# Attention over half batches of queries, interleaved with the feed-forward of the half batch before it

## The chip, the core and the metric

One Trainium2 chip, one of its cores. The metric is device time in microseconds (us), measured on the chip; lower is better. The engines named below are PE (TensorE: matmuls and transposes, with the weight loads as a row of their own), DVE (VectorE), ACT (ScalarE), POOL (GpSimd) and SP (SyncE, which here only issues DMAs). Each has its own queue and works it off in the order of the program.

## The reference

Hashed attention over 4 batches of 8 heads, 768 tokens and 64 channels, and then a gated feed-forward over the 3072 tokens of 512 channels that the heads make together:

```python
# attention: q, k, v (4, 8, 768, 64), proj (64, 6)
q_bits = (einsum('bhsd,dk->bhsk', q, proj) > 0)
k_bits = (einsum('bhsd,dk->bhsk', k, proj) > 0)
mask   = bucket(q_bits)[:, :, :, None] == bucket(k_bits)[:, :, None, :]   # all 6 bits agree
scores = where(mask, q @ k.T / sqrt(64), -1e9)
attn   = softmax(scores) @ v
# feed-forward: x (3072, 512) are the heads side by side
gelu   = gelu_erf(x @ w_gate)              # w_gate (512, 1536)
ffn    = (gelu * (x @ w_val)) @ w_out      # w_val (512, 1536), w_out (1536, 512)
out    = x + sigmoid(x @ w_res) * ffn      # w_res (512, 512)
```

All inputs are float32.

## The kernel before, in words

**Mask inside the matmul.** For each head there is a tile `aug` of 71 rows: 64 rows with the scaled channels of q (first 768 columns) and of k (next 768), 6 rows with the hash bits as +0.5 or -0.5, and a constant row (1 on the q side, -1.5 on the k side). One matmul over 71 rows gives the score plus a term that is zero where all bits agree and large and negative elsewhere, so Exp needs no mask. The constant row is written once by memsets (L82, L83) on DVE into the 12 buffers of `aug`; the memsets cover the bit rows too, which later DMAs overwrite.

**Preparing a pair of heads** (`prep_pair`, 16 pairs in all): POOL casts v into `vaug` (L141); PE transposes q and k in float32 in three groups of four (L148, tile `tps`); ACT copies groups 0 and 2 and DVE group 1 into `trT` (L150, L152); PE multiplies with `proj` (L156, tile `hps`); DVE makes the bits (L159); DVE writes the 64 channel rows of `aug` in bf16 (L163, four operations); SP issues eight small DMAs that move the bits to their rows (L170). Each `yield` ends a part; the main loop takes one part at a time.

**An attention step** (`scores`, then `attend` two steps later, `LEAD`): one block of 128 keys of one head against all 768 queries. PE: 512 + 256 columns into the tile `sc` (L183, L184, two buffers). ACT: Exp of 768 columns into `e` (L186). PE: six matmuls of 65 columns into `av` (L196, one buffer, 64 channels and the softmax sum for six blocks of queries). After the sixth block of keys DVE takes the reciprocal and writes `xtok` (L205, L206). A batch has 48 steps.

**Feed-forward of a batch.** `transpose_x` (PE L215 into `xps`, DVE L216 into `xT`), then all 24 gate groups (PE L223, four matmuls of 384 columns each; ACT Gelu L225) in one block, and then the generator `feed_forward`: for each half of the batch 12 items of `vps` (L233, four matmuls of 384) with a DVE product (L237), and for each of its three token blocks `rps` (L242), Tanh on ACT (L245, the sigmoid), `ops` (L249, twelve matmuls of 512 in three items), two DVE operations (`y` L254, `o` L256) and the output DMA on SP (L257). That makes 48 items. Tiles `tps`, `hps`, `xps`, `gps`, `vps`, `rps` and `ops` share three PSUM buffers.

**Order.** It is written out by hand: the program's order is each engine's order. Two pairs are prepared ahead of the loop. Batch 0's 48 steps have no feed-forward beside them; the weights (14 loads on SP in float32, L133, and a cast on POOL, L134) are brought in here, one in three steps, and the other pairs are prepared. In the steps of a later batch one or two items of the previous batch's `feed_forward` are issued per step, and the next batch's pairs are prepared in every second step. Then follow what is left of the generators, `transpose_x` and the 24 gate groups. The last batch's `feed_forward` comes after all attention.

Of the kernel before, what the change touches and what calls it, by code (L numbers as in the profile page):

```python
# [10 lines left out]
FP32 = mybir.dt.float32  # L11
BF16 = mybir.dt.bfloat16
AF = mybir.ActivationFunctionType
ALU = mybir.AluOpType
PSUM = bass.MemoryType.PSUM
# [3 lines left out]
def kernel(  # L19
# [24 lines left out]
    KAUG = D + NBITS + 1  # L44
# [12 lines left out]
    wstage = ctx.enter_context(tc.tile_pool(name="wstage", bufs=2))  # L57
    tr_pool = ctx.enter_context(tc.tile_pool(name="tr", bufs=2))
    e_pool = ctx.enter_context(tc.tile_pool(name="e", bufs=6))
    x_pool = ctx.enter_context(tc.tile_pool(name="x", bufs=2))  # L60
    h_pool = ctx.enter_context(tc.tile_pool(name="h", bufs=1))
# [5 lines left out]


    ident = const.tile([P, P], FP32, name="ident")
    make_identity(nc, ident)  # L70
    ident_bf = const.tile([P, P], BF16, name="ident_bf")
    make_identity(nc, ident_bf)
    proj_pair = const.tile([P, 32], FP32, name="proj_pair")
    nc.vector.memset(proj_pair, 0.0)
    nc.sync.dma_start(proj_pair[0:D, 0:NBITS], proj)
    nc.sync.dma_start(proj_pair[D:2 * D, NBITS:2 * NBITS], proj)

    NAUG = 12
    augs = []
    for i in range(NAUG):  # L80
        a = const.tile([P, 2 * S], BF16, name=f"aug{i}")
        nc.vector.memset(a[D:KAUG, 0:S], 1.0)  # L82
        nc.vector.memset(a[D:KAUG, S:2 * S], -0.25 * NBITS)  # L83
        augs.append(a)
    NVA = 2
    vaugs = []
    for i in range(NVA):
# [7 lines left out]

    staged = {}

    def load_pair(b, j):
        for nm, src in (("q", q), ("k", k), ("v", v)):
            s = stage.tile([P, 2, T, D], FP32, tag=nm + "s", name=nm + "s")  # L100
            nc.sync.dma_start(
                s, src[b, 2 * j:2 * j + 2].rearrange("h (p t) d -> p h t d", t=T))
            staged[(nm, b, j)] = s
# [6 lines left out]
    def load_weights():  # L110
        for dst, src in ((wg, moe_w_gate), (wv, moe_w_val)):
            for ko in range(KM):
                yield dst[:, ko, :], src[ko * P:(ko + 1) * P, :], None
        for k3 in range(KF // 3):
            yield (wo[:, 3 * k3:3 * k3 + 3, :],
                   moe_w_out[3 * k3 * P:(3 * k3 + 3) * P, :].rearrange("(c p) d -> p c d", p=P), 3)
        for k2 in range(KM // 2):
            yield (wr[:, 2 * k2:2 * k2 + 2, :],
                   moe_w_res[2 * k2 * P:(2 * k2 + 2) * P, :].rearrange("(c p) d -> p c d", p=P), 2)

    weight_gen = load_weights()

    def load_weight():
        nxt = next(weight_gen, None)
        if nxt is None:
            return
        dst, src, parts = nxt
        tmp = wstage.tile([P, DFF], FP32, tag="wtmp", name="wtmp")
        if parts is None:
            view = tmp  # L130
        else:
            view = tmp[:, :parts * DMODEL].rearrange("p (c d) -> p c d", c=parts)
        nc.sync.dma_start(view, src)  # L133
        nc.gpsimd.tensor_copy(dst, view)  # L134


    def prep_pair(b, j):

        qs, ks, vs = (staged.pop((nm, b, j)) for nm in "qkv")
        va = vaugs[b % NVA]  # L140
        nc.gpsimd.tensor_copy(va[:, 2 * j:2 * j + 2, :, 0:D], vs)  # L141
# [17 lines left out]
        nc.vector.tensor_scalar(bits, hp[:, 0:CH], 0.0, 0.5, op0=ALU.is_gt, op1=ALU.subtract)  # L159
        for hh in range(2):  # L160
            a = aug_of(b, 2 * j + hh)
            for par in range(2):
                nc.vector.tensor_scalar_mul(  # L163
                    a[0:D, :].rearrange("d (s n) -> d s n", s=2)[:, :, par * CH:(par + 1) * CH],
                    trT[par * D:(par + 1) * D, hh * S:(hh + 1) * S].rearrange("d (s n) -> d s n", s=2),
                    QKS)
            for side in range(2):
                for par in range(2):
                    row = 32 * (2 * hh + side) + NBITS * par
                    nc.sync.dma_start(  # L170
                        a[D:D + NBITS, side * S + par * CH:side * S + (par + 1) * CH],
                        bits[row:row + NBITS, :])
        yield


    x_tok, xT, gh = {}, {}, {}
    e_tiles, av_tiles = {}, {}

    def scores(b, h, jt):
        a = aug_of(b, h)  # L180
        sp = sc_psum.tile([P, 1024], FP32, tag="sc", name="sc")
        lhsT = a[0:KAUG, S + jt * P:S + (jt + 1) * P]
        nc.tensor.matmul(sp[:, 0:512], lhsT, a[0:KAUG, 0:512], start=True, stop=True)  # L183
        nc.tensor.matmul(sp[:, 512:S], lhsT, a[0:KAUG, 512:S], start=True, stop=True)  # L184
        e = e_pool.tile([P, S], BF16, tag="e", name="e")
        nc.scalar.activation(e, sp[:, 0:S], AF.Exp, scale=EXPS)  # L186
        e_tiles[(b, h, jt)] = e

    def attend(b, h, jt):
        e = e_tiles.pop((b, h, jt))  # L190
        if jt == 0:
            av_tiles[(b, h)] = av_psum.tile([P, 512], FP32, tag="av", name="av")
        av = av_tiles[(b, h)]
        va = vaugs[b % NVA]
        for t in range(T):
            nc.tensor.matmul(av[:, t * DV:t * DV + D + 1], e[:, t * P:(t + 1) * P], va[:, h, TS[jt], :],  # L196
                             start=(jt == 0 and t == 0), stop=(jt == T - 1),
                             skip_group_check=True)
        if jt == T - 1:
            del av_tiles[(b, h)]  # L200
            o = av[:, 0:T * DV].rearrange("p (t d) -> p t d", d=DV)
            if h == 0:
                x_tok[b] = x_pool.tile([P, T, DMODEL], BF16, tag="xtok", name="xtok")
            rec = s_pool.tile([P, T, 1], FP32, tag="rec", name="rec")
            nc.vector.reciprocal(rec, o[:, :, D:D + 1])  # L205
            nc.vector.tensor_mul(x_tok[b][:, :, h * D:(h + 1) * D], o[:, :, 0:D],  # L206
                                 rec.to_broadcast([P, T, D]))


    def transpose_x(b):  # L210
        xT[b] = x_pool.tile([P, KM, S], BF16, tag="xT", name="xT", bufs=1)
        for ko in range(KM):
            ps = mm_psum.tile([P, 1024], BF16, tag="mm", name="xps")
            for t in range(T):
                nc.tensor.transpose(ps[:, t * P:(t + 1) * P], x_tok[b][:, t, ko * P:(ko + 1) * P], ident_bf)  # L215
            nc.vector.tensor_copy(xT[b][:, ko, :], ps[:, 0:S])  # L216

    def gate(b, m, c):
        if m == 0:
            gh[(b, c)] = h_pool.tile([P, KF, CH], BF16, tag="gh", name="gh", bufs=3)  # L220
        ps = mm_psum.tile([P, 512], FP32, tag="mm", name="gps")
        for kk in range(KM):
            nc.tensor.matmul(ps[:, 0:CH], wg[:, kk, m * P:(m + 1) * P], xT[b][:, kk, c * CH:(c + 1) * CH],  # L223
                             start=(kk == 0), stop=(kk == KM - 1))
        nc.scalar.activation(gh[(b, c)][:, m, :], ps[:, 0:CH], AF.Gelu)  # L225

    def feed_forward(b):

        for c in range(2):
            for m in range(KF):  # L230
                ps = mm_psum.tile([P, 512], FP32, tag="mm", name="vps")
                for kk in range(KM):
                    nc.tensor.matmul(ps[:, 0:CH], wv[:, kk, m * P:(m + 1) * P],  # L233
                                     xT[b][:, kk, c * CH:(c + 1) * CH],
                                     start=(kk == 0), stop=(kk == KM - 1))
                sl = gh[(b, c)][:, m, :]
                nc.vector.tensor_mul(sl, ps[:, 0:CH], sl)  # L237
                yield 4 * CH
            for t in range(c * T // 2, (c + 1) * T // 2):
                rps = mm_psum.tile([P, 512], FP32, tag="mm", name="rps")  # L240
                for kk in range(KM):
                    nc.tensor.matmul(rps, xT[b][:, kk, t * P:(t + 1) * P], wr[:, kk, :],  # L242
                                     start=(kk == 0), stop=(kk == KM - 1))
                th = o_pool.tile([P, DMODEL], BF16, tag="th", name="th")
                nc.scalar.activation(th, rps, AF.Tanh, scale=0.5)  # L245
                yield 4 * 512
                ops = mm_psum.tile([P, 512], FP32, tag="mm", name="ops")
                for kk in range(KF):
                    nc.tensor.matmul(ops, gh[(b, c)][:, kk, (t - c * T // 2) * P:(t - c * T // 2 + 1) * P], wo[:, kk, :],  # L249
                                     start=(kk == 0), stop=(kk == KF - 1))  # L250
                    if kk % 4 == 3 and kk < KF - 1:
# [97 lines left out]
```

## Time and profile before

| | |
|---|---|
| median of 3 runs | 469.35 us (466.07 to 469.82) |
| profiled execution | 469.5 us |
| its span, first to last instruction | 467.4 us |
| PE busy | 389.1 us (83%) |
| ACT busy | 237.0 us (51%) |
| DVE busy | 189.8 us (41%) |
| POOL busy | 36.2 us (8%) |
| DMA moved | 36.7 MB, mean 79 GB/s |
| mean granted PE clock | 0.936 |

A row of the profile names the line, the engine, the operation and its tiles (out<-in), with the count, the busy time or start, and in brackets or behind a bar the idle time of the engine just before it and what ended that wait. Matmuls overlap in PE's pipeline, so the time that one takes is read from start to start or from the chain, not from its own duration. "PEclk" is the clock that PE was granted, 1.00 being full speed. A busy PE says nothing by itself; what matters in a stage is what it waits for.

### The profile page before, as it was taken

The page shows a single profiled execution, that of the slowest core. Times are in us where ns is not written, and L with a number is a line of the kernel's source. Part 1 is how long each engine was busy: PE and PEld are TensorE (multiplying, and loading weights), DVE is VectorE, ACT ScalarE, POOL GpSimd, SP SyncE. Part 2 cuts the span into 40 slices and gives each one's busy share as a digit, 9 for nine tenths or more (in the row PEclk, how much of TensorE's full clock was granted, in tenths as well). Part 3 has the DMA queues.
Part 4 walks back from the last instruction along what each step waited for, and adds up shares of the span by engine and source line. Part 5 has one row for each costly group of instructions (what it writes and reads, how often), then busy time and mean ns, then how long its engine had stood idle before and what let it go on. Part 6 is the DMA issues. An engine that isn't in the chain of part 4 may idle for free.

```text
span 467.4 us, 7688 instructions
## 1 busy us (share of the span) xinstructions
PE 389.1 (83%) x3104; PEld 231.1 (49%) x3104; DVE 189.8 (41%) x347; ACT 237.0 (51%) x352; POOL 36.2 (8%) x38
## 2 busy tenths in 40 slices
PE   3115678568899999967999999788999999899996
PEld 2012354335556565545656465465665555556452
DVE  7722344334205466344124664624043543113463
ACT  2003356248675544657575444575765456964101
POOL 1000134223300010000000100100000000000000
PEclk9998787679999999979999999977999999999999
DMA  3030965663600340400200440400000101000101
GB/s 101 0 104 18 377 232 197 240 240 90 242 0 1 126 148 5 169 5 7 101 1 0 128 148 26 150 3 5 0 1 25 45 24 46 1 0 1 39 31 67
DMA packets 21538, 36.73 MB, mean 79 GB/s; under 512 B 2304, under 2 KB 15360, under 8 KB 21504
## 3 DMA queue, kind: packets, MB, share of 16 engines
q1 hardware_dynamic: 21504, 36.25, 22.6%
q8 instruction: 24, 0.39, 0.3%
q14 instruction: 10, 0.08, 0.1%
HBM read 29.36 MB, written 6.29 MB: 76 GB/s over the span
## 4 chain that ended last, share of the span: by engine, by line
PE 68%; DVE 16%; DMA 5%; ACT 5%; issue 3%; SPq 3%; ACTq 0%; DVEq 0%
PE ops L249 13%; PE gps L223 13%; PE vps L233 10%; PE sc L183 7%; PE av L196 7%; PE tps L148 5%; PE rps L242 4%; DMA ks<-in_k_dram 4%; ACT e L186 4%; DVE aug L163 4%; PE sc L184 3%; PE hps L156 3%; DVE xtok L206 3%; SPq L170 2%; DVE aug L83 2%
## 5 line engine op out<-in xcount | busy, mean ns | idle before, releaser
L186 ACT ACTIVATE e<-sc 128x768 bf16<-128x768 f32 x192 | 150.4, 811 | 106.1 <-PE sc L184 106.1
L196 PEld LDWEIGHTS <-e 128*128 128x128 bf16 x1152 | 63.1, 103 | 64.8 <-DVE xtok L206 24.5
L196 PE MATMUL av<-vaug,e 128*128 128x65 bf16 x1152 | 71.7, 202 | 25.3 <-DVE xtok L206 23.8
L237 DVE TENSOR_TENSOR gh<-vps,gh 128x384 bf16<-128x384 f32 x96 | 52.9, 557 | 91.2 <-PE vps L233 87.1
L183 PE MATMUL sc<-aug 71*128 71x512 bf16 x192 | 78.4, 408 | 4.4 <-ACT e L186 3.4
L249 PE MATMUL ops<-wo,gh 128*128 128x512 bf16 x288 | 70.0, 379 | 0.0
L233 PE MATMUL vps<-xT,wv 128*128 128x384 bf16 x384 | 69.8, 326 | 0.1
L223 PE MATMUL gps<-xT,wg 128*128 128x384 bf16 x384 | 64.7, 329 | 0.4 <-DVE xT L216 0.2
L225 ACT ACTIVATE gh<-gps 128x384 bf16<-128x384 f32 x96 | 47.0, 490 | 25.2 <-PE gps L223 25.2
L184 PE MATMUL sc<-aug 71*128 71x256 bf16 x192 | 55.4, 289 | 0.0
L223 PEld LDWEIGHTS <-wg 128*128 128x128 bf16 x384 | 37.8, 99 | 26.3 <-issue 2.4
L233 PEld LDWEIGHTS <-wv 128*128 128x128 bf16 x384 | 37.3, 97 | 24.5 <-issue 0.3
L148 PE MATMUL tps<-ident,qs 128*128 128x128 f32 x96 | 23.6, 341 | 30.6 <-DMA qs<-in_q_dram 30.6
L152 ACT COPY trT<-tps 128x512 f32<-128x512 f32 x32 | 18.7, 584 | 49.6 <-PE tps L148 49.6
L249 PEld LDWEIGHTS <-gh 128*128 128x128 bf16 x288 | 27.9, 97 | 31.0 <-issue 1.2
L163 DVE TENSOR_SCALAR aug<-trT 64x768 bf16<-64x768 f32 x64 | 38.3, 599 | 0.7
L254 DVE SCALAR_TENSOR_TENSOR y<-th,ops 128x512 f32<-128x512 bf16 x24 | 16.5, 688 | 50.7 <-PE ops L249 29.5
L245 ACT ACTIVATE th<-rps 128x512 bf16<-128x512 f32 x24 | 14.3, 597 | 42.2 <-PE rps L242 42.2
L150 DVE COPY trT<-tps 128x512 f32<-128x512 f32 x16 | 11.3, 703 | 55.6 <-PE tps L148 55.4
L148 PEld LDWEIGHTS tps<-ident,qs 128*128 128x128 f32 x96 | 15.2, 177 | 37.1 <-issue 18.8
L141 POOL CAST vaug<-vs 128x768 bf16<-128x768 f32 x16 | 15.1, 944 | 200.9 <-DMA vs<-in_v_dram 150.0
L156 PE MATMUL hps<-trT,proj_pair 128*32 128x384 f32 x128 | 19.5, 572 | 11.0 <-DVE trT L150 11.0
(33 smaller groups left out, 238.9 us busy)
## 6 DMA issues: line engine op xcount, KB each, us to landing
qs<-in_q_dram SPq DMA_DIRECT2D x16, 384.0 KB
ks<-in_k_dram SPq DMA_DIRECT2D x16, 384.0 KB
vs<-in_v_dram SPq DMA_DIRECT2D x16, 384.0 KB
out_dram<-o SPq DMA_DIRECT2D x24, 256.0 KB
wtmp<-in_moe_w_gate_dram SPq DMA_DIRECT2D x4, 768.0 KB
wtmp<-in_moe_w_val_dram SPq DMA_DIRECT2D x4, 768.0 KB
wtmp<-in_moe_w_out_dram SPq DMA_DIRECT2D x4, 768.0 KB
aug<-bits SPq DMA_DIRECT2D x128, 4.5 KB
```

What stands on the lines that cost most here:

```text
L148: nc.tensor.transpose(ps[:, i * P:(i + 1) * P], tiles[4 * g + i], ident)
L156: nc.tensor.matmul(hp[32 * i:32 * i + 32, 0:CH], proj_pair, trT[:, i * CH:(i + 1) * CH], start=True, stop=True)
L163: nc.vector.tensor_scalar_mul(a[0:D, :].rearrange("d (s n) -> d s n", s=2)[:, :, par * CH:(par + 1) * CH], trT[par * D:(par + 1) * D, hh * ...
L183: nc.tensor.matmul(sp[:, 0:512], lhsT, a[0:KAUG, 0:512], start=True, stop=True)
L184: nc.tensor.matmul(sp[:, 512:S], lhsT, a[0:KAUG, 512:S], start=True, stop=True)
L186: nc.scalar.activation(e, sp[:, 0:S], AF.Exp, scale=EXPS)
L196: nc.tensor.matmul(av[:, t * DV:t * DV + D + 1], e[:, t * P:(t + 1) * P], va[:, h, TS[jt], :], start=(jt == 0 and t == 0), stop=(jt == T - 1),
L223: nc.tensor.matmul(ps[:, 0:CH], wg[:, kk, m * P:(m + 1) * P], xT[b][:, kk, c * CH:(c + 1) * CH], start=(kk == 0), stop=(kk == KM - 1))
L225: nc.scalar.activation(gh[(b, c)][:, m, :], ps[:, 0:CH], AF.Gelu)
L233: nc.tensor.matmul(ps[:, 0:CH], wv[:, kk, m * P:(m + 1) * P], xT[b][:, kk, c * CH:(c + 1) * CH], start=(kk == 0), stop=(kk == KM - 1))
L237: nc.vector.tensor_mul(sl, ps[:, 0:CH], sl)
L249: nc.tensor.matmul(ops, gh[(b, c)][:, kk, (t - c * T // 2) * P:(t - c * T // 2 + 1) * P], wo[:, kk, :], start=(kk == 0), stop=(kk == KF - 1))
```

## The change

- **Half batches.** A unit is now half a batch of queries (384) against all 768 keys, eight units in all. A step takes two blocks of keys for 384 queries: two score matmuls of 384 columns into two PSUM banks, one Exp over 2 x 384, six matmuls of 65 columns. `av` holds two heads of three query blocks. A unit has 24 steps.
- **Feed-forward of the unit ahead.** Beside a unit's 24 steps runs the whole `feed_forward` of the unit before it (24 items), paced by a credit (`RATE`, 17/24 per step, against item prices of 0.65 and 0.87). At a unit's end come one more item, `transpose_x`, what is left of the generator and 12 gate groups.
- **Weights** are cast by the DMA that loads them, issued from POOL (13 of them), without a staging tile and without POOL's casts.
- **Constant rows with the bits.** `proj_pair` gets a zero column for a seventh row, and a per-partition `shift` makes it the constant; the eight DMAs per pair move 7 rows in place of 6. The 24 memsets of `aug` are gone, and `aug` has 16 buffers. `shift` is made from the identity by one reduction for each side and two small DVE operations.
- **Start.** q, k and v of pair 0 are the first loads, those of pair 1 follow; `proj` is loaded on ACT's queue; for pair 0, four of the eight bits DMAs are issued by ACT.
- **Preparation.** The channel rows of a head are cast in parts of their own (`cast_aug`), so a pair has six parts. Pairs 2 and 3 begin at steps 1 and 7; batch 1's pairs at steps 24, 30, 36 and 42; those of batches 2 and 3 every 12 steps from the first step of the batch ahead.

```diff
-    for i in range(NAUG):
-        a = const.tile([P, 2 * S], BF16, name=f"aug{i}")
-        nc.vector.memset(a[D:KAUG, 0:S], 1.0)
-        nc.vector.memset(a[D:KAUG, S:2 * S], -0.25 * NBITS)
...
+    load_pair(0)
...
+    nc.scalar.dma_start(proj_pair[0:D, 0:NBITS], proj)
+    nc.scalar.dma_start(proj_pair[D:2 * D, NR:NR + NBITS], proj)
+    load_pair(1)
...
+    nc.vector.tensor_scalar(shift, ind[:, 0:1], -1.5, 0.5, op0=ALU.mult, op1=ALU.add)
+    nc.vector.scalar_tensor_tensor(shift, ind[:, 1:2], 0.25 * NBITS - 0.5, shift,
+                                   op0=ALU.mult, op1=ALU.add)
...
     def load_weights():
         for dst, src in ((wg, moe_w_gate), (wv, moe_w_val)):
             for ko in range(KM):
-                yield dst[:, ko, :], src[ko * P:(ko + 1) * P, :], None
+                nc.gpsimd.dma_start(dst[:, ko, :], src[ko * P:(ko + 1) * P, :])
+                yield
+        nc.gpsimd.dma_start(wr, moe_w_res.rearrange("(c p) d -> p c d", p=P))
+        yield
         for k3 in range(KF // 3):
...
+            nc.gpsimd.dma_start(
+                wo[:, 3 * k3:3 * k3 + 3, :],
+                moe_w_out[3 * k3 * P:(3 * k3 + 3) * P, :].rearrange("(c p) d -> p c d", p=P))
+            yield
...
-        nc.vector.tensor_scalar(bits, hp[:, 0:CH], 0.0, 0.5, op0=ALU.is_gt, op1=ALU.subtract)
+        nc.vector.tensor_scalar(bits, hp[:, 0:CH], 0.0, shift, op0=ALU.is_gt, op1=ALU.subtract)
...
+                    row = 32 * (2 * hh + side) + NR * par
+                    eng = nc.scalar if n == 0 and par == 1 else nc.sync
+                    eng.dma_start(
+                        a[D:KAUG, side * S + par * CH:side * S + (par + 1) * CH],
+                        bits[row:row + NR, :])
...
+    def scores(i):
+        b, c, j, hh, jp = steps[i]
+        a = aug_of(b, 2 * j + hh)
+        sp = sc_psum.tile([P, 2, 512], FP32, tag="sc", name="sc")
+        for x in range(2):
+            jt = 2 * jp + x
+            nc.tensor.matmul(sp[:, x, 0:CH], a[0:KAUG, S + jt * P:S + (jt + 1) * P],
+                             a[0:KAUG, c * CH:(c + 1) * CH], start=True, stop=True)
+        e = e_pool.tile([P, 2, CH], BF16, tag="e", name="e")
+        nc.scalar.activation(e, sp[:, :, 0:CH], AF.Exp, scale=EXPS)
...
+    cast_v(0)
+    drain(prep_pair(0))
+    cast_v(1)
+    drain(prep_pair(1))
+    load_pair(2)
+    load_pair(3)
+    run(weights)
+    run(weights)
+
+    begin = {2: 1, 3: 7}
+    for n in range(4, len(pairs)):
+        b, j = pairs[n]
+        begin[n] = (b - 1) * 2 * LB + (LB + 6 * j if b == 1 else 12 * j)
+    loads = {}
+    for n in range(4, len(pairs)):
+        loads.setdefault(max(2, begin.get(n - 3, -6) + 5), []).append(n)
...
+    RATE = 17.0 / LB
...
+    for i in range(NS + LEAD):
+        if i < NS:
+            scores(i)
+        if i >= LEAD:
+            attend(i - LEAD)
+        for n in loads.pop(i, []):
+            load_pair(n)
+        if i < 14 * 2 and i % 2 == 0:
+            run(weights)
+        if prep is None and todo and i >= begin[todo[0]]:
+            n = todo.pop(0)
+            cast_v(n)
+            prep = prep_pair(n)
+        if prep is not None:
+            if next(prep, "done") == "done":
+                prep = None
+        credit += RATE
+        if credit > 0:
+            credit = fill(credit) if ff is not None else 0.0
+        if i >= LEAD and (i - LEAD) % LB == LB - 1:
+            u = (i - LEAD) // LB
+            fill(0.8)
+            transpose_x(u)
+            fill(100.0)
             for m in range(KF):
...
+                gate(u, m)
+            ff = feed_forward(u)
+            credit = 0.0
+    drain(ff)
```

More of the change, by code (lines that the diff above doesn't have):

```diff
@@ L176 @@
+    steps = [(b, c, j, hh, jp) for b in range(B) for c in range(2) for j in range(NPAIR)
+             for hh in range(2) for jp in range(T // 2)]
+    LB = NPAIR * 2 * (T // 2)
+    LEAD = 2
     x_tok, xT, gh = {}, {}, {}
     e_tiles, av_tiles = {}, {}
[L179 to L207, printed above, removed]
@@ new lines, in attend @@
+    def attend(i):
+        b, c, j, hh, jp = steps[i]
+        u = i // LB
+        e = e_tiles.pop(i)
+        first = hh == 0 and jp == 0
+        last = hh == 1 and jp == T // 2 - 1
+        if first:
+            av_tiles[0] = av_psum.tile([P, 512], FP32, tag="av", name="av")
+        av = av_tiles[0]
+        va = vaugs[b % 2]
+        for x in range(2):
+            jt = 2 * jp + x
+            for t in range(TC):
+                o = (hh * TC + t) * DV
+                nc.tensor.matmul(av[:, o:o + D + 1], e[:, x, t * P:(t + 1) * P],
+                                 va[:, 2 * j + hh, TS[jt], :],
+                                 start=(first and x == 0 and t == 0), stop=(jt == T - 1),
+                                 skip_group_check=True)
+        if last:
+            o = av[:, 0:2 * TC * DV].rearrange("p (h t d) -> p h t d", h=2, d=DV)
+            if j == 0:
+                x_tok[u] = x_pool.tile([P, TC, DMODEL], BF16, tag="xtok", name="xtok")
+            rec = s_pool.tile([P, 2, TC, 1], FP32, tag="rec", name="rec")
+            nc.vector.reciprocal(rec, o[:, :, :, D:D + 1])
+            nc.vector.tensor_mul(
+                x_tok[u][:, :, j * P:(j + 1) * P].rearrange("p t (h d) -> p h t d", h=2),
+                o[:, :, :, 0:D], rec.to_broadcast([P, 2, TC, D]))
@@ L227, in feed_forward @@
-    def feed_forward(b):
-        for c in range(2):
-            for m in range(KF):
[L231 to L251, printed above, removed]
-                        yield 4 * 512
-                y = o_pool.tile([P, DMODEL], FP32, tag="y", name="y")
-                nc.vector.scalar_tensor_tensor(y, th, 1.0, ops, op0=ALU.add, op1=ALU.mult)
-                o = o_pool.tile([P, DMODEL], FP32, tag="o", name="o")
-                nc.vector.scalar_tensor_tensor(o, y, 0.5, x_tok[b][:, t, :], op0=ALU.mult, op1=ALU.add)
-                nc.sync.dma_start(
-                    out[b * S:(b + 1) * S, :].rearrange("(p t) d -> p t d", t=T)[:, TS[t], :], o)
-                yield 4 * 512
```

233 lines of the change are left out of this document (117 added, 116 removed).

## The prediction

> **What bounds the kernel now.** I read the page's slices first, then cut the span into the kernel's own stages, then took unit prices from the chain and the timeline. The first fence is the TensorE (PE) row of the slices, the second the stages (columns: window, length, busy time and count for PE, weight loads, DVE, ACT, POOL, then granted clock, DMA share, GB/s).
>
> ```profile
> PE   3115678568899999967999999788999999899996
> ```
> ```profile
> 0.00:23.60 23.60, 5.97 (x20) 2.66 (x20) 18.29 (x30) 2.46 (x3) 1.96 (x9) 1.00 0.15 50
> 38.20:123.25 85.05, 57.74 (x533) 36.54 (x532) 32.45 (x61) 44.24 (x61) 24.24 (x19) 0.80 0.60 211
> 139.50:198.70 59.20, 58.45 (x490) 33.83 (x488) 31.56 (x58) 32.09 (x45) 2.21 (x2) 1.00 0.27 89
> 198.70:224.08 25.38, 18.66 (x193) 13.09 (x191) 11.41 (x23) 15.18 (x20) 0.98 (x1) 0.80 0.10 32
> 340.50:391.90 51.40, 50.57 (x404) 28.60 (x403) 22.75 (x42) 27.65 (x36) 0.00 (x0) 1.00 0.07 27
> 391.90:411.14 19.24, 15.78 (x205) 10.33 (x202) 6.25 (x14) 16.03 (x21) 0.00 (x0) 1.00 0.04 15
> 426.40:467.40 41.00, 36.49 (x193) 18.58 (x190) 21.27 (x36) 4.07 (x7) 0.00 (x0) 0.98 0.11 39
> ```
>
> Where attention and feed-forward are interleaved (139.50 to 198.70, 340.50 to 391.90), PE is busy 98% at a clock of 1.00: nothing but PE work counts there. It isn't the limit in three other kinds of stage: the start (nothing is scored before 38), batch 0's attention, which has no feed-forward to stand beside (85 us), and the leftover of each later batch, whose feed-forward has run out before its 48 attention steps have (25 and 19 us). The tail is PE work without attention.
>
> Now prices at full clock. The rows are the chain's (start, length, what), then PE's timeline, then ACT's and one group of the table by lines.
>
> ```profile
> 72.81 0.94 PE hps L156 x8
> ```
> ```profile
> 350.25 1.30 PE vps L233 x8
> 351.55 0.18 PE av L196 x6
> 351.74 0.22 PE sc L183
> 351.95 0.11 PE sc L184
> 352.06 0.86 PE rps L242 x4
> ```
> ```profile
> 411.14 15.27 PE gps L223 x93
> ```
> ```profile
> 74.67 0.49 PE L148 MATMUL tps<-ident,qs 128*128 128x128 f32 x3
> 75.00 0.27 PE L148 MATMUL tps<-ident,ks 128*128 128x128 f32 x1
> 75.11 0.26 PE L196 MATMUL av<-vaug,e 128*128 128x65 bf16 x3
> ```
> ```profile
> 402.54 2.96 ACT L186 ACTIVATE e<-sc 128x768 bf16<-128x768 f32 x4
> ```
> ```profile
> L225 ACT ACT_TABLE_LOAD x4 | 5.1, 1283 | 0.1
> ```
>
> An attention step costs PE 0.18 + 0.22 + 0.11 = 0.51 us and ACT 2.96/4 = 0.74. Four vps matmuls are 0.65, four rps or ops matmuls 0.86, one gate group 4 x 15.27/93 = 0.66. Four transposes take 75.11 - 74.67 = 0.44, so a pair's preparation is 3 x 0.44 + 0.94 = 2.26. Checked on 340.50 to 391.90: 24 vps items (15.6), 24 items of four wide matmuls (20.6) and 27 or 28 steps (14) sum to 50 against 51.4, so I add 2% to what I sum in this way. Alone, attention runs at ACT's 0.74 and leaves PE a third idle; beside 0.7 us of feed-forward per step it is free for ACT. That is what the change trades on.
>
> **The change part by part.** Matmul work is unchanged: a step has 384 + 384 columns in place of 512 + 256 and six narrow matmuls as before. What moves is order.
>
> *Start.* Rows of PE, DVE and SP:
>
> ```profile
> 5.60 0.87 PE L148 MATMUL tps<-ident,qs 128*128 128x128 f32 x3 [5.60 <-DMA qs<-in_q_dram]
> ```
> ```profile
> 21.48 1.50 PE L156 MATMUL hps<-trT,proj_pair 128*32 128x384 f32 x6 [11.03 <-DVE trT L150]
> 32.95 0.87 PE L148 MATMUL tps<-ident,qs 128*128 128x128 f32 x3 [9.97 <-DMA qs<-in_q_dram]
> ```
> ```profile
> 36.03 2.24 PE L156 MATMUL hps<-trT,proj_pair 128*32 128x384 f32 x8
> 38.20 0.61 PE L183 MATMUL sc<-aug 71*128 71x512 bf16 x1
> ```
> ```profile
> 19.68 0.70 DVE L83 MEMSET aug<- 7x768 bf16 x1
> 20.54 0.89 DVE L150 COPY trT<-tps 128x512 f32<-128x512 f32 x1 [0.16 <-issue]
> ```
> ```profile
> 2.20 0.59 SPq L101 DMA_DIRECT2D qs<-in_q_dram  x1
> ```
> ```profile
> 23.62 5.82 SPq L170 DMA_DIRECT2D aug<-bits  x8
> 29.49 0.45 SPq L101 DMA_DIRECT2D qs<-in_q_dram  x1
> ```
>
> The first trT copy on DVE stands behind 24 memsets until 20.54; the constant rows now come with the bits, so they go. With q issued first (some 1.45 us earlier), pair 0's transposes and copies end near 8.2, hps at 9.8 (1.50), bits at 10.4. The new reduce, shift and identity copy are five small DVE operations ahead of that, beside the wait for q, and cost nothing unless they exceed 4 us. Pair 1 is already loaded. Its first ACT copy waits behind the four bits DMAs that ACT now issues (4 x 5.82/8 = 2.9, to 13.3); then hps (2.24): first scores at 16 in place of 38.2.
>
> What is late next is SP's queue. Pair 1's eight bits DMAs hold it from 16.5 to 22.3, and only behind them stand the loads of pairs 2 and 3, then 4. Issue to use was 32.95 - 29.49 = 3.46, so pair 2's q is there at 25.8 and k a microsecond later. PE has its transposes queued right behind the second scores, and everything behind them waits: PE stands some 8 us, and unit 0 goes on at 26.8. From there ACT sets the pace: 22 x 0.74, four trT copies of 0.58, two last attends 1.5, that is 45. Pair 3's bits are issued behind pair 2's bits and a load of 1.2 MB, which I take to cost 4 to 6 more. Attention of unit 0 ends at t1 = 51. Bounds: 42 without any of these waits but half the load's; 66 at batch 0's present pace (85.05/48 = 1.77 a step, 22 steps from 26.8).
>
> *Weights.* SP loses 14 weight loads and POOL the casts; 10.5 MB now go through DMAs that POOL issues. Three are issued at 12, the others behind the cast of pair 2's v at 28. No casting DMA is in the trace. The nearest rows are the plain loads:
>
> ```profile
> q1 hardware_dynamic: 21504, 36.25, 22.6%
> ```
> ```profile
> GB/s 0 0 0 0 3 2 18 157 332 366 375 369 323 335 89 0 0 0 0 0 0 0 0 0 0 0 0 0 0 0 0 0 0 0 0 0 0 0 0 0
> ```
>
> At the 350 GB/s of those slices the 8.1 MB left at 28 with 3.5 MB of pairs 3 to 5 end at 61; wg is there by 36, wv by 48. The gates start at 53, vps at 61, ops near 77: nothing waits. The first row gives the other end: 0.226 x 16 x 467.4 us / 21504 = 79 ns for a packet of 1.7 KB. If a casting DMA moves 512-byte packets at that price, the weights take 20480 x 79/16 = 101 us, wo lands near 130 (with 17 us for the pairs' loads), and ops waits 53 us. I take the first, since the bytes read are the same and rows of 2 to 6 KB make larger packets possible, and keep the second as a case.
>
> ```profile
> L163 DVE TENSOR_SCALAR aug<-trT x64: 541/555/1725, 23.5 to 316.3; 64x768 bf16<-64x768 f32 x64
> ```
>
> The row (least, median, longest ns) shows DVE's casts stretched by up to 1.17 us, in the stretch where POOL casts weights. [...]
>
> *Boundaries between units.* There were four, now eight.
>
> ```profile
> 408.24 1.17 PE L215 MATMUL xps<-ident_bf,xtok 128*128 128x128 bf16 x18
> ```
> ```profile
> 408.67 0.56 DVE L206 TENSOR_TENSOR xtok<-av,rec 128x384 bf16<-128x384 f32 x1
> 409.15 1.94 DVE L216 COPY xT<-xps 128x768 bf16<-128x768 bf16 x4
> ```
> ```profile
> 463.10 0.69 DVE L254 SCALAR_TENSOR_TENSOR y<-th,ops 128x512 f32<-128x512 bf16 x1 [2.04 <-PE ops L249]
> 463.82 0.69 DVE L256 SCALAR_TENSOR_TENSOR o<-y,xtok 128x512 f32<-128x512 f32 x1
> ```
>
> The yielded prices give 23 of 24 feed-forward items before the boundary and the last in the 0.8 filled there, so reciprocal and xtok are covered by two items (1.7). But this last item also issues y and o, ahead of the xT copies on DVE. PE ends the 12 transposes after 0.7 (12 x 0.06) while DVE needs 0.69 + 0.69 + 0.55 before the first gate and 0.55 more before its third matmul: PE stands 1.8 us. ACT takes 16 table loads in place of 8 (four for Gelu and as many for Exp, now twice that); 8 x 1.28 = 10 us, off the path: a unit has 24 x 0.74 + 12 x 0.49 + 3 x 0.60 + 2 x 1.28 = 28 us of ACT in 41.
>
> [...] In 391.90 to 411.14 PE has 3.5 us of such gaps and the clock stays 1.00. [...]
>
> *The av buffer.* One buffer: after each pair the next av waits for reciprocal and xtok (0.2 + 0.56 and two handovers, about 1.0). Between them stand one item (0.65 or 0.86) and scores (0.33): covered, where DVE isn't held by y and o. By the credits no pair ends there. Taken as 0; the bound is 1 us at 28 pair ends.
>
> **Sum.** t1 51; first boundary 1.7 + 0.7 and 12 gates 7.9: 10. Seven units of 24 x 0.51 = 12.2, feed-forward 12 x 0.65 + 12 x 0.86 = 18.1, transposes 0.7, gap 1.8, gates 7.9: 40.7, times 7 is 285. Twelve preparations x 2.26 = 27. The 2% on these, 6. Last feed-forward 18.1 and from y's start at 463.10 to the span's end 467.4, 4.3: 22.4. Together 401. The profiled execution took 469.5 against its span of 467.4, and the median is 469.35, so 2 us come on top: **403**.
>
> **Rivals.** *Slower: starved by the casting DMA.* If it moves 256-byte packets at 79 ns, weights take 202 us, wo lands near 231 against 77, and the time is 403 + 154 = 557. It passes the time of before once ops waits 66 us, at packets under about 450 bytes. Against: 2 to 6 KB rows. For: no row shows such a DMA. 0.06. The same with 512 bytes: 403 + 53 = 456; 0.08.
>
> *Start as slow as now.* Batch 0's attention ran at a clock of 0.80 with waits for loads and bits, and the same SP queue remains: t1 = 66, time 418. 0.14.
>
> *Pair ends wait for av.* 28 x 1 us: 431. For: 198.70 to 224.08 loses time of this kind. Against: there no feed-forward stands between. 0.10.
>
> *Better:* t1 = 42 and no 2%: 388. 0.10. *It does not do what it says* (units wait on a buffer so that little overlaps): within 1% of before; 0.02.
>
> **How the numbers follow.** The forecast (393 to 412) has 0.50. From 386 to 436 stand it, the slow start, the waits for av and half of the better case: about 8 in 10. Its own range is 393 to 412. A measurement of this kernel tells 1% (5 us) from no change. Faster by over 1%: 0.92; same 0.02; slower 0.06.
>
> **What would show it.** First scores near 16 and PE waiting for pair 2's q until 26; the first gate at 52 to 54 with no wait for wg; seven units of 41 to 50 us with PE over 93% busy at a clock of 1.00; a gap under 2 us ahead of each unit's gates, ended by an xT copy; 8 loads of the Gelu table; one feed-forward, 18 us, behind the last gates. PE waiting for wg, wv or wo proves the slow weights; PE waiting for xtok some 28 times proves the pair ends; a first gate after 60 with weights landed proves the slow start.

## The result and the profile after

The changed kernel takes 412.76 us (median of 4 runs, 411.62 to 414.89) against 469.11 (the kernel before, median of 4 runs); the ratio is 0.8815, 95% interval 0.8759 to 0.8871. The forecast was 403 in a range of 386 to 436; the narrower 393 to 412, to which the prediction gave an even chance, ends just below the result. The profiled execution took 411.9 us, its span is 410.1. In e6 and in e9 below one run of the four was over 1.5% above the fastest; the ratios leave it out, the medians do not.

The page's slices of the changed kernel, PE's busy share and its granted clock:

```profile
PE   5348589999989998999989998999999999998995
PEclk9658859999999999999999999999999999999999
```

PE is now full from the seventh slice on to the tail, at full clock. What isn't full is the first 64 us. The same span by stages (window, length, busy time and count of PE, weight loads, DVE, ACT, POOL, then clock, DMA share, GB/s): start, the wait for pair 2, the rest of unit 0's attention, then units cut from one gate block to the next:

```profile
0.00:16.00 16.00, 8.14 (x40) 4.25 (x40) 5.64 (x15) 3.53 (x5) 4.07 (x11) 0.94 0.67 187
16.00:26.80 10.80, 2.24 (x9) 0.93 (x7) 2.74 (x5) 1.51 (x2) 0.00 (x0) 0.50 0.56 146
26.80:61.80 35.00, 26.02 (x229) 17.12 (x229) 9.30 (x18) 20.58 (x28) 10.31 (x15) 0.70 1.07 262
64.18:115.18 51.00, 48.20 (x417) 29.46 (x421) 27.22 (x50) 32.54 (x49) 4.05 (x4) 1.00 0.33 107
115.18:161.30 46.12, 44.54 (x392) 27.91 (x396) 22.65 (x44) 31.45 (x46) 1.00 (x2) 1.00 0.21 72
...
298.24:339.00 40.76, 39.22 (x345) 23.75 (x348) 14.50 (x29) 29.06 (x41) 0.00 (x0) 1.00 0.05 20
339.00:379.04 40.04, 38.51 (x342) 23.31 (x345) 14.51 (x29) 27.55 (x39) 0.00 (x0) 1.00 0.06 21
379.04:410.10 31.06, 26.20 (x143) 13.98 (x143) 11.24 (x19) 7.68 (x15) 0.00 (x0) 1.00 0.09 34
```

The units are where the sum had them: with four preparations 51.0 (forecast 40.7 + 4 x 2.26 and 2%: 50.7), with two 46.1 (46.1), with none 40.8 and 40.0 (41.5). The leftover stages of before, 25 and 19 us, are gone. PE's waits in the table of waits (total, times, longest):

```profile
PE tps L155 <- DMA qs<-in_q_dram: 12.6, 2, 8.6
...
PE gps L262 <- DVE xT L254: 10.4, 8, 1.4
...
PE sc L210 <- DMA aug<-bits: 5.5, 1, 5.5
...
PE av L230 <- DVE xtok L240: 3.9, 5, 1.6
```

No row has PE waiting for wg, wv, wo or wr. The first gate stands at 64.18 where the sum had it at 53.4. These 10.8 us are the error; the seven units and the tail behind them gave 2.5 back. The chain ahead of that gate (start, length, what) shows the bits of pair 3 (chain rows of under 0.1 us lie between these):

```profile
43.31 0.74 SPq L173
44.10 0.70 SPq L173
44.86 8.07 DMA aug<-bits
52.97 0.82 PE sc L210 x2
```

### The profile page after: what moved, and what is told of

The parts are those of the page before. It is cut to its first block, busy times and chain, and to the rows that moved or that the text cites. A ratio compares the mean times of both kernels' runs of the same rounds, so it can differ in the third digit from the quotient of the medians.

```text
span 410.1 us, 7658 instructions
## 1 busy us (share of the span) xinstructions
PE 366.4 (89%) x3077; PEld 222.5 (54%) x3104; DVE 171.6 (42%) x328; ACT 248.6 (61%) x360; POOL 22.9 (6%) x35
## 3 DMA queue, kind: packets, MB, share of 16 engines
q1 hardware_dynamic: 18248, 25.84, 18.4%
q0 software_dynamic: 3280, 5.24, 7.1%
## 4 chain that ended last, share of the span: by engine, by line
PE 80%; DVE 10%; DMA 4%; SPq 2%; issue 2%; ACTq 1%; ACT 0%; DVEq 0%
PE gps L262 16%; PE ops L287 14%; PE sc L210 14%; PE vps L272 13%; PE av L230 8%; PE tps L155 6%; PE rps L280 5%; PE hps L163 4%; DVE aug L191 2%; DMA aug<-bits 2%; DMA ks<-in_k_dram 2%; DVE gh L275 2%; SPq L173 2%; DVE y L292 1%; DVE o L294 1%
## 5 line engine op out<-in xcount | busy, mean ns | idle before, releaser
L213 ACT ACTIVATE e<-sc 128x768 bf16<-128x768 f32 x192 | 153.3, 811 | 73.4 <-PE sc L210 72.9
L210 PE MATMUL sc<-aug 71*128 71x384 bf16 x384 | 98.8, 340 | 6.6 <-DMA aug<-bits 5.5
L272 PE MATMUL vps<-xT,wv 128*128 128x384 bf16 x384 | 75.2, 326 | 0.0
L262 PE MATMUL gps<-xT,wg 128*128 128x384 bf16 x384 | 64.8, 326 | 10.4 <-DVE xT L254 10.4
L230 PE MATMUL av<-vaug,e 128*128 128x65 bf16 x1152 | 68.5, 197 | 4.2 <-DVE xtok L240 3.9
L210 PEld LDWEIGHTS <-aug 71*128 71x128 bf16 x384 | 37.2, 102 | 37.1 <-DMA aug<-bits 5.6
L272 PEld LDWEIGHTS <-wv 128*128 128x128 bf16 x384 | 33.2, 98 | 18.8 <-issue 3.8
L287 PEld LDWEIGHTS <-gh 128*128 128x128 bf16 x288 | 25.3, 98 | 24.1 <-issue 3.1
L292 DVE SCALAR_TENSOR_TENSOR y<-th,ops 128x512 f32<-128x512 bf16 x24 | 16.5, 688 | 45.8 <-PE ops L287 40.8
L155 PE MATMUL tps<-ident,qs 128*128 128x128 f32 x96 | 21.2, 311 | 12.6 <-DMA qs<-in_q_dram 12.6
L143 POOL CAST vaug<-vs 128x768 bf16<-128x768 f32 x16 | 14.2, 887 | 206.3 <-DMA vs<-in_v_dram 158.9
L280 PE MATMUL rps<-wr,xT 128*128 128x512 bf16 x84 | 23.4, 379 | 0.5
L166 DVE TENSOR_SCALAR bits<-hps,shift 128x384 bf16<-128x384 f32 x16 | 9.9, 617 | 30.1 <-PE hps L163 29.3
L155 PE MATMUL tps<-ident,ks 128*128 128x128 f32 x96 | 20.8, 306 | 0.5 <-DMA ks<-in_k_dram 0.4
```

Of the source, the lines that this page charges most:

```text
L155: nc.tensor.transpose(ps[:, i * P:(i + 1) * P], tiles[4 * g + i], ident)
L210: nc.tensor.matmul(sp[:, x, 0:CH], a[0:KAUG, S + jt * P:S + (jt + 1) * P], a[0:KAUG, c * CH:(c + 1) * CH], start=True, stop=True)
L213: nc.scalar.activation(e, sp[:, :, 0:CH], AF.Exp, scale=EXPS)
L230: nc.tensor.matmul(av[:, o:o + D + 1], e[:, x, t * P:(t + 1) * P], va[:, 2 * j + hh, TS[jt], :], start=(first and x == 0 and t == 0), stop ...
L280: nc.tensor.matmul(rps, xT[u][:, kk, t * P:(t + 1) * P], wr[:, kk, :], start=(kk == 0), stop=(kk == KM - 1))
L287: nc.tensor.matmul(ops, gh[u][:, kk, t * P:(t + 1) * P], wo[:, kk, :], start=(kk == 0), stop=(kk == KF - 1))
```

## The experiments

Times are medians of 4 runs each; the ratios refer to runs of the kernel before that were taken beside each (medians 468.7 to 469.6). "First gate" is the start of unit 0's gates in the one profiled execution. In the runs that leave the start alone the first scores came between 16.0 us (the changed kernel) and 18.1 (e3), so a difference of 1 or 2 us between two first gates can be the start's and not the edit's.

| run | us | ratio (95%) | first gate |
|---|---|---|---|
| changed kernel | 412.8 | 0.882 (0.876 to 0.887) | 64.2 |
| e1 no interleaving | 463.6 | 0.985 (0.979 to 0.991) | 64.8 |
| e2 memsets back | 427.9 | 0.911 (0.908 to 0.913) | 80.4 |
| e8 weights by SP and POOL's casts | 422.7 | 0.899 (0.895 to 0.903) | 74.0 |
| e3 pair 5's load at step 11 | 413.3 | 0.879 (0.876 to 0.883) | 65.3 |
| e9 pair 5's load at step 12 | 410.0 | 0.872 (0.867 to 0.876) | 61.6 |
| e4 wv, wr, wo from 48 us | 409.6 | 0.870 (0.866 to 0.874) | 63.5 |
| e10 wv, wr, wo after step 21 | 407.1 | 0.868 (0.864 to 0.872) | 61.4 |
| e5 pair 2 loaded first | 408.8 | 0.871 (0.869 to 0.873) | 60.7 |
| e11 PE kept busy in the wait | 413.4 | 0.878 (0.874 to 0.883) | 66.4 |
| e12 e10 and e11 | 405.7 | 0.867 (0.864 to 0.870) | 57.9 |
| e6 transposes ahead of the last item | 401.2 | 0.856 (0.853 to 0.858) | 64.0 |
| e7 four edits together | 385.4 | 0.819 (0.815 to 0.823) | 50.0 |

### What the parts of the change are worth

**e1, no interleaving.**

```diff
-    RATE = 17.0 / LB
+    RATE = 0.0
```

> The credit is 0 per step, so no feed-forward item stands beside attention: each unit's 24 items come in one block at the boundary. Theory 'overlap' (attention alone runs at ACT's 0.74 us a step and leaves PE a third idle, the items fill it): each of seven units loses 24 x (0.74 - 0.51) = 5.5 us, 39 in all, and some 10 more at pair ends, where av waits for xtok; preparations then hide in PE's idle time, up to -20. Time 413 + 30 to 50, so 440 to 460, with PE waiting for av's release about 28 times. Theory 'order is worth nothing, the gain is the start': within 5 us of 413.

463.6, 51 us slower than the changed kernel and above the expected 440 to 460. Without overlap the other edits leave 1.5% against before. That isn't the share of overlap in the 56 us gained: e1 takes away also the interleaving that the kernel before had, and e2 and e8 below give 15 and 10 us for other parts. One unit without preparations by stages (from the end of its gates to the next gates, then a stretch of its attention), and two of the kernel's waits, ACT's Exp and the release of av:

```profile
333.30:378.70 45.40, 42.80 (x301) 24.49 (x300) 13.39 (x26) 23.87 (x30) 0.00 (x0) 0.74 0.03 12
...
345.00:360.00 15.00, 14.43 (x110) 8.58 (x109) 2.47 (x7) 10.82 (x14) 0.00 (x0) 0.50 0.01 2
```
```profile
PE sc L210 <- ACT e L213: 10.0, 23, 1.7
...
PE av L230 <- DVE xtok L240: 9.5, 20, 1.4
```

PE waited for av's release 20 times. By the starts of the gate blocks in the two chains, the five units with preparations lost 4.0 to 6.9 us each, at a mean clock of 0.92 to 0.97 in windows of 44 to 49 us of the first three, and near the 5.5 of ACT's pace. The two without preparations lost 12.5 and 11.5: their attention was granted half the clock for most of its time (0.66 from 333.3 to 345 and 0.50 from 345 to 360 in the first; in the second the chain's steps come 0.97 us apart, as in the first), so that PE, 96% busy, and not ACT set its pace. That is why it cost more than the expected 39.

**e2, the memsets back.**

```diff
-    augs = [const.tile([P, 2 * S], BF16, name=f"aug{i}") for i in range(NAUG)]
+    augs = []
+    for i in range(NAUG):
+        a = const.tile([P, 2 * S], BF16, name=f"aug{i}")
+        if i < 12:
+            nc.vector.memset(a[D:KAUG, 0:S], 1.0)
+            nc.vector.memset(a[D:KAUG, S:2 * S], -0.25 * NBITS)
+        augs.append(a)
```

> 24 memsets of the bit and constant rows of 12 aug buffers stand at DVE's head again; everything else stays, the bits DMAs still move 7 rows. Theory 'start counts in full': the first DVE copy of trT goes from 6.4 to about 21, the first scores from 16 to about 31 and the end by as much: 413 + 14 = 427. Theory 'DMA fills unit 0 anyway' (the DMA engines are busy at 0.99 from 28 to 61 and set the first gate): most of the delay is absorbed, under 6 us: at most 419.

427.9: the delay at the start reaches the end in full. First scores, by PE's timeline, and the first gates, by the chain:

```profile
31.33 1.46 PE L216 MATMUL sc<-aug 71*128 71x384 bf16 x4
```
```profile
80.44 8.10 PE gps L268 x48
```

16.03 became 31.33 and 64.18 became 80.44. Unit 0 is one chain from its first load on, and DMA traffic hides none of it.

**e8, weights as before.**

```diff
+        tmp = wstage.tile([P, DFF], FP32, tag="wtmp", name="wtmp")
...
+        nc.sync.dma_start(view, src)
+        nc.gpsimd.tensor_copy(dst, view)
...
-                nc.gpsimd.dma_start(dst[:, ko, :], src[ko * P:(ko + 1) * P, :])
+                weight(dst[:, ko, :], src[ko * P:(ko + 1) * P, :], None)
...
```

> Weights as in the kernel before: loaded in float32 on SP into two staging tiles and cast by POOL; all else as changed. Theory 'the casting DMA is worth its place' (14 loads and their waits for a staging tile stand on SP between bits and pair loads): bits and pairs come later, wv and wo come later still, first gate 5 to 25 us later: 418 to 440. Theory 'same bytes, same time' (the HBM bytes read are the same, 10.5 MB): within 4 us of 413.

422.7. The casting DMA is worth 10 us, and not for its bytes read, which are the same: SP's queue, with 14 loads and their waits for a staging tile in it, brings bits late. PE's wait for bits grew from 5.5 to 12.6 us, 7.1 of the 9.8 by which the first gate came later:

```profile
PE sc L219 <- DMA aug<-bits: 12.6, 2, 10.6
```

### Why unit 0 ended 11 us late

**e3 and e9, pair 5's load behind pair 3's bits** (11 in e3, 12 in e9).

```diff
-        loads.setdefault(max(2, begin.get(n - 3, -6) + 5), []).append(n)
+        loads.setdefault(11 if n == 5 else max(2, begin.get(n - 3, -6) + 5), []).append(n)
```

> Pair 5's three loads are issued behind pair 3's bits on SP, not ahead of them. In the changed kernel these bits land at 52.97, 9.7 us after their first issue, and PE stands 5.5 us. Theory 'same ring' (the bits queue behind pair 5's 1.2 MB in SP's own DMA queue, which lands at 52.4): bits land by 47, the first gate moves from 64.2 to 56 to 59, time 405 to 408. Theory 'weights' (all DMA engines are taken by the casting DMAs, whatever stands ahead in SP's queue): bits land at 51 to 53 as now, time within 2 us of 413.

e3 missed its aim: a preparation ends with a yield of its own, so pair 3's bits go out in step 11, behind the loads of that step. So the order on SP is that of the changed kernel, and e3 says nothing between the theories; its first gate comes 1.1 us later behind first scores that came 2.1 later. e9 moves the load:

> The edit of the load5 run, done one step later: a pair's preparation takes seven steps and not six, so pair 3's bits are issued at step 11, and only from step 12 are pair 5's loads behind them on SP. Theory 'same ring' (bits queue behind pair 5's 1.2 MB): bits land 2 to 3 us after their issue, PE's wait of 4 to 5.5 us goes, first gate at 58 to 60, time 406 to 409. Theory 'turns' (in each DMA engine the casting DMAs take turns with SP's queue, and a turn of theirs lasts long, so each of four small DMAs waits whatever stands ahead in its own queue): bits land 6 to 8 us after issue as now, time 411 to 414.

410.0, the first gate 2.6 us earlier, and 1.8 us of waiting for bits are left of 5.5. That lies between the two theories: the load ahead in SP's queue has a part, though not all of it.

**e4 and e10, the weights later** (the diff is e10's; e4 has at step 25 the cast of pair 5's v, moved up, in place of the copy).

```diff
+    go = const.tile([P, 1], BF16, name="go")
...
-        if i < 14 * 2 and i % 2 == 0:
+        if i in (0, 2):
             run(weights)
+        if i == 22:
+            nc.gpsimd.tensor_copy(go, e_tiles[21][:, 0, 0:1])
+            drain(weights)
```

> POOL issues the nine DMAs of wv, wr and wo behind the casts of v of pairs 4 and 5 (about 46 us), not at 29 to 39. wv is used from 73 us, wo from 93. Both theories of the late bits (same ring: pair 5's load, without the weights beside it, lands by 46; weights: the engines are free) give bits by 47 to 48 and the first gate at 56 to 59: 405 to 408. Theory 'neither, the bits' landing has its own latency': no change, 413. If wv or wo arrive too late, PE waits for them ahead of vps or ops and the gain is lost.

> POOL issues wv, wr and wo only when the Exp of step 21 is done, by one copy of one column that reads it: by then all bits of pair 3 have landed. Pair 5's load stays ahead of pair 3's bits. Theory 'turns': both waits for bits in unit 0 vanish (4 bits after the load of 3.5 us), first gate at 56 to 59, wv lands some 11 us after the copy, 61 to 64, before vps: time 404 to 407. Theory 'same ring': pair 5's load, alone on the engines, lands in 4 us: the same 404 to 407. Theory 'the weights have no part in it' (the run with weights from 48 us gained 3 us only): 409 to 413.

e4's 409.6 is between its theories too. There POOL reached the weights at 48.2, while the last bits were being issued. POOL's timeline and the chain there:

```profile
47.43 0.83 POOL L143 CAST vaug<-vs 128x768 bf16<-128x768 f32 x1 [8.77 <-DMA vs<-in_v_dram]
48.20 2.18 POOL L128 DMA_DIRECT2D wv<-in_moe_w_val_dram  x4
```

```profile
49.08 0.69 SPq L173
...
49.82 5.56 DMA aug<-bits
...
55.42 0.76 PE sc L210 x2
```

Pair 5's load had landed by 47.4, where the cast of its v starts, so nothing stood ahead of these bits on SP, and 5 KB still took 5.6 us while casting DMAs ran. In e10 no weights run at that time, pair 5's load is issued ahead of the bits as in the changed kernel, and the wait is gone:

```profile
PE sc L211 <- DMA aug<-bits: 0.5, 1, 0.5
```

The chains of e9 and of e10 give the time that the bits on which PE waited took to land:

```profile
45.23 4.77 DMA aug<-bits
```
```profile
50.80 2.88 DMA aug<-bits
```

With the casting DMAs and the load of pair 5 ahead it was 8.07 (the changed kernel), with the casting DMAs alone 4.77 (e9) and 5.56 (e4), with the casting DMAs held back 2.88 (e10). So the DMAs that are cut loose early delay the bits by some 2 to 3 us, and a load that stands ahead on the same queue beside them adds about as much; whether the bits wait for turns with the casting DMAs, as one theory of e9 has it, no run shows. But e10's first gate came only to 61.4, not to 56 to 59: with the bits there, something else set the pace (1.2 us of it is a later start, first scores at 17.3).

**e11 and e12, PE kept busy in the wait.**

```diff
+    fillb = const.tile([P, 512], BF16, name="fillb")
+    nc.gpsimd.memset(fillb, 0.5)
...
+            if n == 2:
+                wps = mm_psum.tile([P, 512], FP32, tag="mm", name="wps")
+                for _ in range(28):
+                    nc.tensor.matmul(wps, ident_bf, fillb, start=True, stop=True)
             cast_v(n)
```

> 28 matmuls of 512 columns on constant data, read by nobody, stand on PE right ahead of pair 2's first transposes, where PE waits 8.5 us for q; nothing else changes. Theory 'clock' (after that wait PE works at a granted 0.50 to 0.62 and not ACT's 0.74 us but PE's half-speed 1.8 us a step sets the pace of unit 0): the clock is up from about 24, steps 2 to 4 fall from 1.8 to 1.2 us or less, first gate 2 to 4 us earlier (60 to 62). Theory 'DMA' (bits and loads alone set unit 0's end): steps are faster but the wait for pair 3's bits grows by as much, first gate at 64 as before and time 411 to 414.

> The 28 filler matmuls ahead of pair 2's transposes, together with wv, wr and wo held back until the Exp of step 21. Alone, the second gave 407.1 with steps at half clock after the wait, and the first 413.4, its faster steps lost to a longer wait for pair 3's bits. Theory 'one limit behind the other' (with the bits' wait gone, PE's half clock sets the pace of unit 0): now the faster steps reach the end, first gate at 56 to 59 in place of 61.4, time 402 to 405. Theory 'the clock is no limit at all': 407 within 2 us, first gate at 61.

PE's timeline behind the wait, first in the changed kernel and then in e11:

```profile
26.04 0.90 PE L155 MATMUL tps<-ident,qs 128*128 128x128 f32 x3 [8.56 <-DMA qs<-in_q_dram]
27.02 0.47 PE L155 MATMUL tps<-ident,ks 128*128 128x128 f32 x1
27.29 0.84 PE L210 MATMUL sc<-aug 71*128 71x384 bf16 x2
27.93 0.54 PE L230 MATMUL av<-vaug,e 128*128 128x65 bf16 x6
28.28 0.67 PE L155 MATMUL tps<-ident,ks 128*128 128x128 f32 x2
28.74 0.64 PE L155 MATMUL tps<-ident,qs 128*128 128x128 f32 x2
29.17 0.85 PE L210 MATMUL sc<-aug 71*128 71x384 bf16 x2
```
```profile
27.89 0.49 PE L212 MATMUL sc<-aug 71*128 71x384 bf16 x2
28.22 0.34 PE L232 MATMUL av<-vaug,e 128*128 128x65 bf16 x6
28.40 0.41 PE L157 MATMUL tps<-ident,ks 128*128 128x128 f32 x2
28.65 0.38 PE L157 MATMUL tps<-ident,qs 128*128 128x128 f32 x2
28.86 0.49 PE L212 MATMUL sc<-aug 71*128 71x384 bf16 x2
```

From one step's scores to the next: 29.17 - 27.29 = 1.88 us, and 0.97 with the clock up. Yet e11 took 413.4: its faster steps met pair 3's bits no earlier, and one wait grew from 5.5 to 7.7 us. With the weights held back as well (e12) the first gate comes to 57.9, 3.5 ahead of e10's, as "one limit behind the other" had it. In time that is 405.7 (expected: 402 to 405) against 407.1, and the runs of e10 spread over 404.6 to 409.6, so the gain in the whole is not resolved; in the profiles it is.

**e5, pair 2 loaded first.**

```diff
     load_pair(1)
+    load_pair(2)
...
-    load_pair(2)
     load_pair(3)
```

> Pair 2 is loaded right behind pair 1, ahead of all bits DMAs on SP. Theory 'SP's order' (PE stands 8.6 us for pair 2's q only because the load is issued behind pair 1's bits): PE goes on at 17.5 in place of 26, and the first gate comes up to 8.6 us earlier, 404 to 407. Theory 'DMA-bound unit 0' (the engines carry weights and pairs until 61 whatever the order): the wait moves to the bits of pairs 2 and 3, gain under 3 us: 410 to 413.

408.8, 4.0 us less, half of the 8.6. PE goes on at once (pair 2's transposes at 16.99 in place of 26.04), and then one wait for bits takes 7.0 us. Neither theory alone: the order on SP holds the start, DMA traffic what follows.

### The boundary, and a faster version

**e6, transposes ahead of the last item.**

```diff
-            fill(0.8)
             transpose_x(u)
             fill(100.0)
```

> At a unit's end the transposes come first, and the last feed-forward item (with y and o) stands behind them, so that PE works while DVE copies xT. Theory 'y and o ahead of the copies' (PE waits 1.4 us for xT ahead of seven of the eight gate blocks, 10.4 us in all): PE stands for xtok a little (0.2 to 0.5) but not for xT, 413 - 6 to 9: 404 to 407. Rival: the wait for reciprocal and xtok ahead of the transposes, now covered by one item only, takes as much as it frees: 411 to 414.

401.2, 11.6 us less, more than expected. The gates' wait for xT goes from 10.4 to:

```profile
PE gps L262 <- DVE xT L254: 0.3, 1, 0.3
```

and PE doesn't wait for xtok in its place:

```profile
PE av L230 <- DVE xtok L240: 3.7, 5, 1.4
```

as in the changed kernel (3.9, 5 times). A unit with no preparation is 39.1 and 38.4 us in place of 40.8 and 40.0. Of the 10.4 us of waiting 0.7 stood ahead of unit 0's gates, where e6 changes nothing, so the seven other waits are 9.7 of the 11.2 us by which the seven units got shorter. Another 0.8 lies inside the gate blocks: by the starts of PE's matmuls, the third one, the first that reads the second copy of xT, comes 0.30 us behind the second in the changed kernel, and in e6 0.16 in six of the seven units.

**e7, four edits.** e6, e5, e10, and pair 4's load at step 5, pair 5's at step 12 and pair 6's at step 13.

> Four edits together: transposes ahead of the last item at each boundary (measured alone 401.2), pair 2 loaded behind pair 1 (408.8), wv, wr and wo issued after the Exp of step 21 (407.1), pair 4's loads behind pair 2's bits and pair 5's behind pair 3's (pair 5's alone 410). If the three edits of unit 0 add up (12 us) it is 413 - 12 - 12 = 389; if they free the same wait, 413 - 12 - 6 = 395; if PE waits for wv, above 400.

385.4, ratio 0.819: 6.6% below the changed kernel, and below the 389 of a plain sum. The first and the last gate block in the chain:

```profile
49.97 8.10 PE gps L264 x48
...
353.66 7.80 PE gps L264 x48
```

Unit 0 is 14.2 us shorter, the seven others and the tail 11.5.

## Why the prediction held, point by point

- **What bounds before, and what overlap buys: right.** The seven units and the tail came to 314.9 + 23 us from the end of the first gate block, against 318 + 22.4. Together the unit prices, read from a few rows, were good to 1%. e1 shows what it costs to have nothing beside attention.
- **Start: right.** First scores at 16.03 (forecast 16); PE standing for pair 2's q until 26.04 (25.8); e2 shows that the memsets alone were 15 us.
- **Weights: right.** The queue rows of the changed kernel:

```profile
q1 hardware_dynamic: 18248, 25.84, 18.4%
q0 software_dynamic: 3280, 5.24, 7.1%
```

  The casting DMAs (q0) took 0.071 x 16 x 410.1 = 466 us of engine time by their packets, 29 us of all sixteen, for 10.5 MB read: 360 GB/s, against the 350 taken. It is a rough figure, since the packets of the queues overlap (a DMA share of 1.18 in a stage shown below). A packet is 1.6 KB on the written side, not 512 bytes, so the two starvation rivals fell. The weights were never waited for. But their traffic had a price at another place, the bits.
- **The step that failed: "from there ACT sets the pace: 22 x 0.74".** From 27.29 (step 2) to 46.78 (step 17) 15 steps took 19.5 us, where 15 x 0.74 and four copies make 13.4: 6.1 us. The wait for pair 3's bits was 5.5, as the "4 to 6" had it, but the sum left less for it: 26.8 and the terms listed make 46.9 and not the 45 that is written, so that t1 = 51 holds 4.1 for the bits. From step 18 at 52.97 to the last attend at 62.2 it took 9.3 instead of 5.9: 3.4 us. Add 0.5 for the restart and 1.4 for the bits, take off 0.5 by which the boundary was shorter, and these are, but for rounding, the 10.8 that the first gate came late. The first stretch ran at half clock in part, the second nearly throughout, as the clock column says:

```profile
17.50:26.00 8.50, 0.00 (x0) 0.00 (x0) 1.40 (x3) 0.90 (x2) 0.00 (x0) 0.50 0.42 111
26.00:33.00 7.00, 6.88 (x46) 4.62 (x47) 0.88 (x2) 3.51 (x5) 4.31 (x8) 0.62 1.07 388
...
47.30:52.90 5.60, 0.15 (x5) 0.02 (x1) 0.00 (x0) 0.87 (x2) 0.54 (x1) 0.60 1.18 258
52.90:62.50 9.60, 9.20 (x72) 6.10 (x73) 0.95 (x3) 6.69 (x9) 1.13 (x2) 0.52 0.86 211
```

  How much the clock is worth in the first one, e12 measures. Its window from step 2 to step 17:

```profile
28.62:44.53 15.91, 13.35 (x158) 8.77 (x156) 8.09 (x16) 12.63 (x19) 2.13 (x3) 1.00 0.68 208
```

  At a clock of 1.00 the same 15 steps took 15.9 us, so 3.6 of the 6.1 are the clock. The other 2.5 are there at full clock too: PE stood 1.16 us for xtok at the first pair end in that window, and at the second 0.68 in the changed kernel, which the sum took as 0, and in steps with transposes PE needs 0.98 us (0.51 + 0.44 and the 2%, or 28.62 to 29.60 in e12), more than ACT's 0.74. The second stretch also holds the first transposes of pair 4 (0.9 us), which the sum had among the twelve preparations.

  The prediction had forecast an 8 us wait of PE and then priced the steps behind it at full clock; the 1.00 that it had read in 391.90 to 411.14 stood beside gaps of 3.5 us in all. In the changed kernel the granted clock was 0.50 to 0.62 behind the waits of 8.6 and 5.5 us and 1.00 at the boundaries, behind gaps of up to 1.4, but the long waits don't account for all of it. Cut where the granted clock changed, unit 0 begins so:

```profile
14.23:31.30 17.07, 8.43 (x41) 4.45 (x40) 3.43 (x6) 4.06 (x7) 2.89 (x5) 0.50 0.74 217
31.30:38.13 6.83, 4.98 (x61) 3.11 (x60) 3.86 (x7) 4.63 (x7) 4.29 (x6) 1.00 1.09 269
38.13:41.54 3.41, 3.41 (x24) 2.61 (x22) 0.69 (x1) 2.26 (x4) 1.59 (x2) 0.50 1.08 213
```

  The clock was down already at 14.23, behind a wait of 3.5 us for ACT's copy, ahead of the wait for q. And it fell again at 38.13, where PE's longest wait in the 6.83 us before was 1.6.
- **The rivals.** "Start as slow as now" had t1 at 66 and 418; t1 came to 62, so this case, at 0.14, was nearer to the truth than the forecast in that stage, and the whole fell between the two, nearer to it (418) than to 403. That the forecast came within 10 us is in part luck: the units gave 2.5 us back. Waits for av at pair ends: 3.9 us in all; that rival fell, though 2.6 of them stand in unit 0.
- **Boundaries: right in kind, a little low in size.** 1.4 us of waiting each, 1.8 forecast, but e6 frees 1.6 per unit (11.2 in seven).

Open: why attention alone stays at half clock, and why the clock fell at 38.13; whether the bits wait for turns with the casting DMAs or for engines that are simply full; and the 0.7 us that e6 frees beyond the waits and the third matmuls.

## What to carry to other kernels

Put the work of one stage beside another whose engine is different, and price the pair by chain rows at full clock; such sums were good to 1% here in the seven units, where PE stood 1.4 us at the most and the clock was 1.00, and not in unit 0, where it stood 8.6 and 5.5 us and the clock behind these waits was 0.50 to 0.62. Where a forecast contains such a long wait of PE, price what follows it at half clock, and in a stage of attention alone (0.50 in e1, 0.52 in the changed kernel) take the full clock as the better case. And a DMA that is free of waits goes out as early as its queue comes to it: those of wv were issued from 29.3 us on, for matmuls that began at 73.1. Tie bulk transfers to the moment they are needed, because small ones on which PE waits pay for them (bits that landed in 8.07 us, and in 2.88 with the weights held back).

## What was not expected of the hardware

A 5 KB transfer within SBUF took 4.8 (e9) to 5.6 us (e4) to land while casting DMAs were in flight, and 8.1 with a load ahead of it on its queue. By the profile's packet times, which overlap, a casting packet took 142 ns (466 us / 3280) for 1.6 KB written, and one of SP's queue 0.184 x 16 x 410.1 / 18248 = 66 ns for 1.4 KB moved. And a busy PE is no sign of a full clock: attention alone was granted 0.50 for 15 us in e1 with PE 96% busy, and 0.52 from 52.9 to 62.5 in the changed kernel (9.20 of 9.60 us busy). What kept it there no run shows.
